# Seven-product groups of a squared-ReLU layer: another order of the sums of quarters and of the matmuls around each read of a partial sum

**Chip, cores, metric.** One core of one Trainium2 chip (trn2). The metric is the device time of one execution in microseconds (us), medians of several runs; lower is better.

## The reference

```python
def _attn_ref(x, filt_r, filt_i):                  # x: 8 x 3008 x 256
    X = np.fft.rfft(x, axis=1)
    Y = X * (filt_r + 1j * filt_i)[None]
    return np.fft.irfft(Y, n=x.shape[1], axis=1).astype(np.float32)

def _moe_ref(x, w_in, w_out):                      # x: 24064 x 256, d_ff 2048
    h = np.maximum(x @ w_in, 0.0)
    return (h * h @ w_out).astype(np.float32)
```

A filter in the frequency domain along the sequence, then a layer with squared ReLU. The output is float32.

## The kernel before

The layer runs over 47 groups (0 to 46) of 512 tokens. Each group has eight steps. A step makes two 128-row blocks of h by four matmuls of 512 columns (**first product**, L562), ScalarE takes the ReLU out of PSUM (L566) and VectorE squares it (L570). The **second product** of a group runs in the eight steps of the next group, behind each step's first product, and so do the parts of the Fourier transform of a later batch. For groups 40 to 45 the second product isn't made plainly (64 matmuls of 256 columns) but as a 2 x 2 product of quarters by seven products P1 to P7 (Strassen's scheme in Winograd's form), of 16 matmuls of 128 columns each: 7/8 of the work, for four sums of quarters of h on VectorE.

```python
    # p_x16 has 4 buffers, PSUM tag psO 2; a11..a22 are the quarters of h in SBUF (float16)
    def sums(g, k):                       # called in step k of the next group, on VectorE
        a11, a12, a21, a22 = quads(g)
        if k == 0:
            t = p_x16.tile([128, 8, D], F16, tag="x16", name=f"s3_{g}")
            nc.vector.tensor_sub(out=t, in0=a11, in1=a21)
            sg[g] = {1: a11, 2: a12, 4: a22, 5: a21, 7: t}
        elif k == 1:
            nc.vector.tensor_add(out=a21, in0=a21, in1=a22)
        elif k == 2:
            t = p_x16.tile([128, 8, D], F16, tag="x16", name=f"s2_{g}")
            nc.vector.tensor_sub(out=t, in0=a21, in1=a11)
            sg[g][6] = t
        elif k == 4:
            ...                           # t = a12 - sg[g][6], operand of P3

    # which matmuls of which product stand behind which step: (product, from, to)
    PARTS = (((1, 0, 16),), ((2, 0, 14),), ((2, 14, 16), (5, 0, 8), (6, 0, 4)),
             ((6, 4, 16), (5, 8, 10)), ((5, 10, 16), (7, 0, 8)), ((7, 8, 16),), ((4, 0, 16),),
             ((3, 0, 16),))

    def products(g, k):                   # part k, one step later than sums
        f = sg[g]
        for p, m0, m1 in PARTS[k]:
            ...                           # f["x"], f["y"]: two PSUM tiles of tag psO
            o = f["x"][:, 0] if p in (1, 6, 7, 4) else f["y"][:, 0 if p == 2 else 1]
            for m in range(m0, m1):
                q, t = divmod(m, 2)
                nc.tensor.matmul(o[:, t, :], f[p][:, q, 128*t:128*t+128], sg["w"][p][:, q, :],
                                 start=(m == 0 and p in (1, 2)), stop=(q == 7), ...)
            if m1 < 16:
                continue
            if p == 1:   nc.scalar.copy(out=f["pu"][:, 0], in_=o)      # partial sum read
            elif p == 6: nc.scalar.copy(out=f["u2"], in_=o)            # partial sum read
            elif p == 7:
                nc.scalar.copy(out=f["pu"][:, 1], in_=o)               # partial sum read
                ...                                                    # tiles top, bot
                nc.vector.tensor_add(out=f["top"][..., 0:128], in0=f["y"][:, 0], in1=f["pu"][:, 0])
                nc.vector.tensor_add(out=f["bot"][..., 128:256], in0=f["y"][:, 1], in1=f["pu"][:, 1])
            elif p == 4: ...              # ScalarE: bot[..., 0:128] = o; store
            elif p == 3: ...              # VectorE: top[..., 128:256] = o + u2; store

    for s in range((NG + 1) * SLOTS):     # NG = 47 groups, SLOTS = 8 steps
        g, k = divmod(s, SLOTS)
        if g < NG: ffn_g1(g, k)           # first product and ReLU
        ...
        if (s - 1) // SLOTS - 1 in SEVEN: products((s - 1) // SLOTS - 1, (s - 1) % SLOTS)
        ...                               # plain second product for the other groups
        if g - 1 in SEVEN: sums(g - 1, k)
        if g < NG: ffn_sq(g, k)           # square
```

P1, P6, P7 and P4 add one after the other into the same PSUM region and are read in between: the next may not add before ScalarE has copied what is there. P2 is alone in its region; P3 adds onto P5.

## Time and profile before

| | before |
|---|---|
| time, median (range, 4 runs) | 793.6 us (793.36 to 793.72) |
| TensorE busy, VectorE, ScalarE | 98%, 74%, 70% of the span |
| steady late group, P6 to the next group's P6 | 13.86 us |
| of that, TensorE's work by its issue rate | 13.17 us |

The third row is the distance between equal rows of TensorE's timeline; the fourth counts matmuls times their distance from start to start. The lines are in the prediction. In them L638, L641, L644 and L648 are the four sums in VectorE's queue; L666 is every matmul of the seven products; L676 and L678 are ScalarE's copies behind P6 and P7; L681, L682 and L687 are VectorE's adds (top, bot, top).

### The profile page before, as it was taken

How to read it: one execution, taken by the hardware profiler on the slowest of the kernel's cores; microseconds unless marked ns; L12 is line 12 of the kernel's file. 1: busy time of each engine (PE TensorE's matmuls, PEld its weight loads, DVE VectorE, ACT ScalarE, POOL GpSimd, SP SyncE). 2: the span in 40 equal slices, each digit the busy share in tenths (PEclk: the TensorE clock that was granted, in tenths of full speed). 3: DMA queues.
4: the chain of work that ended last, by engine and by line, in shares of the span. 5: the costliest groups of instructions: out<-in, count | busy, mean ns of one | idle time of the engine just before them, and what ended most of it. 6: DMA issues, size and time to landing. Idle time of an engine off the chain costs nothing.

```text
span 793.1 us, 15477 instructions
## 1 busy us (share of the span) xinstructions
PE 778.2 (98%) x6390; PEld 553.3 (70%) x6390; DVE 584.3 (74%) x943; ACT 558.6 (70%) x723; POOL 23.6 (3%) x36
## 2 busy tenths in 40 slices
PE   8989999999999999999999999999999999999998
PEld 5846667667676676867777677776767667676666
DVE  6856995579855897559965699556995579778773
ACT  3966777777777676767777677676777777776663
POOL 3800000000000000000000000000000000000000
PEclk9999999999999999999999999999999999999999
DMA  9994554345724467155472555524663332511011
GB/s 362 368 260 139 146 158 121 88 132 161 195 65 109 158 165 181 39 170 140 129 177 57 171 146 147 121 75 153 158 178 88 94 133 67 139 36 54 29 54 54
DMA packets 88574, 107.36 MB, mean 135 GB/s; under 512 B 6336, under 2 KB 79040, under 8 KB 84288
## 3 DMA queue, kind: packets, MB, share of 16 engines
q1 hardware_dynamic: 88296, 106.19, 46.8%
q8 instruction: 50, 0.82, 0.4%
q10 hardware_dynamic: 144, 0.18, 0.1%
q14 instruction: 20, 0.16, 0.1%
q0 software_dynamic: 64, 0.00, 0.0%
HBM read 58.12 MB, written 48.23 MB: 134 GB/s over the span
## 4 chain that ended last, share of the span: by engine, by line
PE 86%; DVE 10%; ACT 2%; DMA 1%; issue 0%; SPq 0%; ACTq 0%; DVEq 0%
PE psH L562 36%; PE psO L579 34%; PE psA L361 3%; DVE h L570 2%; PE psY L532 2%; PE psB L445 2%; PE psP L496 2%; PE psX L666 2%; DVE prod L453 2%; ACT h L566 1%; PE psY L666 1%; PE warm L268 1%; DVE s L644 1%; DVE h L641 1%; DVE s L638 1%; DMA zt<-dZ 1%
## 5 line engine op out<-in xcount | busy, mean ns | idle before, releaser
L566 ACT ACTIVATE h<-psH 128x1024 f16<-128x1024 f32 x376 | 384.9, 1025 | 186.6 <-PE psH L562 183.4
L562 PE MATMUL psH<-yt,sWin 128*128 128x512 f16 (+7 forms) x1728 | 387.4, 351 | 1.4 <-DVE yt L541 0.7
L579 PE MATMUL psO<-sWout,h 128*128 128x256 f16 x2624 | 339.2, 272 | 0.6 <-DVE h L570 0.6
L579 PEld LDWEIGHTS <-h 128*128 128x128 f16 x2624 | 253.2, 98 | 65.9 <-DVE h L570 0.9
L570 DVE TENSOR_TENSOR h<-h 128x1024 f16<-128x1024 f16 x376 | 251.8, 684 | 63.2 <-ACT h L566 62.5
L562 PEld LDWEIGHTS <-sWin 128*128 128x128 f16 x1728 | 157.8, 98 | 101.0 <-issue 3.8
L453 DVE TENSOR_TENSOR prod<-psB,sF 128x1024 f16<-128x1024 f32 x84 | 102.3, 1218 | 2.8 <-PE psB L445 2.8
L541 DVE CAST yt<-psY 128x376 f16<-128x376 f32 x62 | 34.0, 549 | 56.8 <-PE psY L532 56.6
L367 DVE CAST u<-psA 96x512 f16<-96x512 f32 x50 | 34.3, 687 | 47.3 <-PE psA L361 45.1
L498 ACT CAST ze<-psP 128x512 f16<-128x512 f32 x84 | 49.1, 585 | 17.2 <-PE psP L496 14.7
L590 ACT COPY ost<-psO 128x512 f32<-128x512 f32 (+1 forms) x84 | 48.8, 581 | 7.9 <-DMA out_dram<-bot 4.3
L532 PE MATMUL psY<-sC,zt 112*128 112x94 f16 x512 | 43.1, 207 | 1.6 <-DMA zt<-dZ 1.6
L532 PEld LDWEIGHTS <-zt 112*128 112x128 f16 x512 | 35.5, 99 | 11.7 <-issue 1.8
L467 DVE TENSOR_TENSOR yf<-prod,yf 128x512 f16<-128x512 f16 x84 | 35.7, 425 | 2.9
L361 PE MATMUL psA<-x,sC 94*96 94x512 f16 x96 | 36.6, 382 | 0.0
L445 PE MATMUL psB<-ut,sSB 128*128 128x256 f16 x192 | 36.5, 273 | 0.0
L539 ACT CAST yt<-psY 128x376 f16<-128x376 f32 x66 | 30.9, 468 | 2.8 <-issue 2.0
L496 PE MATMUL psP<-yf,sSP 128*128 128x256 f16 x168 | 32.1, 272 | 0.5 <-DVE prod L453 0.3
L445 PEld LDWEIGHTS <-sSB 128*128 128x128 f16 x192 | 18.4, 98 | 19.5
L666 PEld LDWEIGHTS <-h 128*128 128x128 f16 x384 | 24.0, 98 | 7.6 <-issue 2.0
L340 DVE CAST x<-x 94x2048 f16<-94x2048 f32 x24 | 29.2, 1216 | 0.0
L365 ACT CAST u<-psA 96x512 f16<-96x512 f32 x50 | 28.6, 572 | 0.0
(88 smaller groups left out, 394.0 us busy)
## 6 DMA issues: line engine op xcount, KB each, us to landing
x<-in_x_dram SPq DMA_DIRECT2D x20, 768.0 KB
zt<-dZ SPq DMA_DIRECT2D x64, 192.0 KB
dU<-u SPq DMA_DIRECT2D x28, 384.0 KB
dZ<-ze SPq DMA_DIRECT2D x28, 384.0 KB
out_dram<-ost SPq DMA_DIRECT2D x58, 128.0 KB
ut<-dU SPq DMA_DIRECT2D x7, 1024.0 KB
out_dram<-ost SPq DMA_DIRECT2D x27, 256.0 KB
xw<-in_x_dram SPq DMA_DIRECT2D x6, 1024.0 KB
```

What stands on the lines that cost most here:

```text
L361: nc.tensor.matmul(ps[0:96, :], sSA, x16s[(b, c)][:, m, :], start=True, stop=True)
L445: nc.tensor.matmul(ps[:, i * D:(i + 1) * D], sSB[:, 2 * p + i, :], uts[b][:, 2 * p + i, :], start=True, stop=True)
L453: nc.vector.tensor_mul(out=prod, in0=ps.rearrange("p (a d) -> p a d", d=D).unsqueeze(1).to_broadcast([128, 2, 2, D]), in1=sF[:, :, 2 * p:2 ...
L496: nc.tensor.matmul(ps[:, i * D:(i + 1) * D], sSP[:, 2 * p + i, :], yf[:, i, :], start=True, stop=True)
L498: nc.scalar.copy(out=zes[(b, c)][:, 2 * i6:2 * i6 + 2, :], in_=ps.rearrange("p (a d) -> p a d", d=D))
L532: nc.tensor.matmul(ps[:, 94 * jj:94 * jj + 94], zt[:, 4 * (g % 2) + jj, dt * 128:(dt + 1) * 128], sSY, start=True, stop=True)
L562: nc.tensor.matmul(ps[:, i, o:o + n], sWin[:, dt, jt * 128:(jt + 1) * 128], yts[b][:, dt, r:r + n], start=(dt == 0), stop=(dt == 1))
L566: nc.scalar.activation(out=h2[:, 2 * s:2 * s + 2, :], in_=ps, func=AF.Relu)
L570: nc.vector.tensor_mul(out=v, in0=v, in1=v)
L579: nc.tensor.matmul(pso[g][:, t % 2, :], h2s[g][:, jt, t * 128:(t + 1) * 128], sWout[:, jt, :], start=(jt == 0), stop=(jt == NJT - 1))
L590: nc.scalar.copy(out=ost[:, h0:h0 + step, :], in_=pso[g][:, h0:h0 + step, :])
L666: nc.tensor.matmul(o[:, t, :], f[p][:, q, 128 * t:128 * t + 128], sg["w"][p][:, q, :], start=(m == 0 and p in (1, 2)), stop=(q == 7), skip ...
```

## The change

Its intent: P5's and P6's sums are to be ready earlier, by making a21+a22 first (in a buffer of its own, since a21 is still needed), and behind each read of a partial sum other matmuls are to stand in TensorE's program ("fillers"), so that ScalarE's copy is over when the region is needed again. The VectorE adds move from P7 to P2, which now ends last of the two.

```diff
         if k == 0:
-            t = ...; nc.vector.tensor_sub(out=t, in0=a11, in1=a21)      # operand of P7
+            nc.vector.tensor_add(out=t, in0=a21, in1=a22); f[5] = t     # t: a new tile each time
         elif k == 1:
-            nc.vector.tensor_add(out=a21, in0=a21, in1=a22)             # operand of P5, in place
+            nc.vector.tensor_sub(out=t, in0=f[5], in1=a11); f[6] = t
         elif k == 2:
-            t = ...; nc.vector.tensor_sub(out=t, in0=a21, in1=a11)      # operand of P6
+            nc.vector.tensor_sub(out=t, in0=a11, in1=a21); f[7] = t
 ...
-    PARTS = (((1, 0, 16),), ((2, 0, 14),), ((2, 14, 16), (5, 0, 8), (6, 0, 4)),
-             ((6, 4, 16), (5, 8, 10)), ((5, 10, 16), (7, 0, 8)), ((7, 8, 16),), ((4, 0, 16),),
-             ((3, 0, 16),))
+    PARTS = (((1, 0, 16),), ((2, 0, 12), (5, 0, 2)), ((5, 2, 8), (6, 0, 8)),
+             ((6, 8, 16), (5, 8, 14)), ((5, 14, 16), (7, 0, 16)), ((2, 12, 16), (4, 0, 8)),
+             ((4, 8, 16), (3, 0, 4)), ((3, 4, 16),))
 ...
             elif p == 7:
                 nc.scalar.copy(out=f["pu"][:, 1], in_=o)
+            elif p == 2:
                 f["top"] = ...; f["bot"] = ...; (the two tensor_add)
```

More of the change, by code (lines that the diff above doesn't have):

```diff
@@ L633, in sums @@
     def sums(g, k):
+        if k not in (0, 1, 2, 4):
+            return
         a11, a12, a21, a22 = quads(g)
         if k == 0:
-            t = p_x16.tile([128, 8, D], F16, tag="x16", name=f"s3_{g}")
-            nc.vector.tensor_sub(out=t, in0=a11, in1=a21)
-            sg[g] = {1: a11, 2: a12, 4: a22, 5: a21, 7: t}
-        elif k == 1:
-            nc.vector.tensor_add(out=a21, in0=a21, in1=a22)
-        elif k == 2:
-            t = p_x16.tile([128, 8, D], F16, tag="x16", name=f"s2_{g}")
-            nc.vector.tensor_sub(out=t, in0=a21, in1=a11)
-            sg[g][6] = t
-        elif k == 4:
-            t = p_x16.tile([128, 8, D], F16, tag="x16", name=f"s4_{g}")
-            nc.vector.tensor_sub(out=t, in0=a12, in1=sg[g][6])
-            sg[g][3] = t
-    PARTS = (((1, 0, 16),), ((2, 0, 14),), ((2, 14, 16), (5, 0, 8), (6, 0, 4)),
-             ((6, 4, 16), (5, 8, 10)), ((5, 10, 16), (7, 0, 8)), ((7, 8, 16),), ((4, 0, 16),),
-             ((3, 0, 16),))
+            sg[g] = {1: a11, 2: a12, 4: a22}
+        f = sg[g]
+        t = p_x16.tile([128, 8, D], F16, tag="x16", name=f"sum_{g}_{k}")
+        if k == 0:
+            nc.vector.tensor_add(out=t, in0=a21, in1=a22)
+            f[5] = t
+        elif k == 1:
+            nc.vector.tensor_sub(out=t, in0=f[5], in1=a11)
+            f[6] = t
+        elif k == 2:
+            nc.vector.tensor_sub(out=t, in0=a11, in1=a21)
+            f[7] = t
+        else:
+            nc.vector.tensor_sub(out=t, in0=a12, in1=f[6])
+            f[3] = t
+    PARTS = (((1, 0, 16),), ((2, 0, 12), (5, 0, 2)), ((5, 2, 8), (6, 0, 8)),
+             ((6, 8, 16), (5, 8, 14)), ((5, 14, 16), (7, 0, 16)), ((2, 12, 16), (4, 0, 8)),
+             ((4, 8, 16), (3, 0, 4)), ((3, 4, 16),))
     def products(g, k):
```

## The prediction

> **What bounds the kernel now.** I read the page first, then the chain of work that ended last, then each engine's timeline of one late group.
>
> The page, part 1 and part 4:
>
> ```profile
> PE 778.2 (98%) x6390; PEld 553.3 (70%) x6390; DVE 584.3 (74%) x943; ACT 558.6 (70%) x723; POOL 23.6 (3%) x36
> ...
> PE 86%; DVE 10%; ACT 2%; DMA 1%; issue 0%; SPq 0%; ACTq 0%; DVEq 0%
> ```
>
> TensorE is 98% busy and 86% of the chain, so most of the time nothing but fewer matmuls can help. But 10% of the chain is on VectorE. In the chain by order of time, nearly all of that lies after 698 us, in the six late groups (40 to 45) whose second product is made of seven products of quarters, the only part that the change touches. Call them P1 to P7; each has 16 matmuls of 128 columns, in eight parts, one behind each of the eight first-product steps of the next group.
>
> TensorE's timeline of one such group in its steady state (start, length, engine, line, op, operands, count, idle):
>
> ```profile
> 733.15 0.40 PE L666 MATMUL psX<-sT,s 128*128 128x128 f16 x4 [0.30 <-DVE s L644]
> 733.39 1.03 PE L562 MATMUL psH<-yt,sWin 128*128 128x512 f16 x4
> ...
> 737.54 0.61 PE L666 MATMUL psX<-sT,s 128*128 128x128 f16 x8
> 737.99 1.03 PE L562 MATMUL psH<-yt,sWin 128*128 128x512 f16 x4
> 739.08 1.05 PE L666 MATMUL psX<-sT,h 128*128 128x128 f16 x16
> ...
> 745.99 0.28 PE L666 MATMUL psY<-sWout,h 128*128 128x128 f16 x2
> 746.10 0.61 PE L666 MATMUL psY<-sT,h 128*128 128x128 f16 x8
> 747.01 0.40 PE L666 MATMUL psX<-sT,s 128*128 128x128 f16 x4 [0.30 <-DVE s L644]
> ```
>
> Here starts are to be read, not lengths, since ends are modelled and overlap. From 733.15 to 747.01 one group takes 13.86 us. The work: four 512-column matmuls take 0.865 us from start to next start, so 32 take 6.92; 12 of 128 columns take 0.67, so 112 take 6.25. Sum 13.17. The other 0.69 us is two holes. The first: the eight of P5 start at 746.10 and would be issued by 746.55 (8 x 0.0557), but P6 starts at 747.01: 0.46 us. The second: the first-product step of 737.99 is issued by 738.85, but P4 starts at 739.08: 0.23 us. The profile doesn't mark this second hole as idle at all, because the modelled end (739.02) covers it.
>
> What ends the first hole, VectorE's timeline:
>
> ```profile
> 741.93 0.42 DVE L687 TENSOR_TENSOR top<-psY,u 128x256 f32<-128x256 f32 x1 [1.13 <-PE psY L666]
> 742.27 1.21 DVE L638 TENSOR_TENSOR s<-h 128x2048 f16<-128x2048 f16 x1
> 743.40 0.68 DVE L570 TENSOR_TENSOR h<-h 128x1024 f16<-128x1024 f16 x1
> 744.00 1.22 DVE L641 TENSOR_TENSOR h<-h 128x2048 f16<-128x2048 f16 x1
> 745.14 0.68 DVE L570 TENSOR_TENSOR h<-h 128x1024 f16<-128x1024 f16 x1
> 745.74 1.22 DVE L644 TENSOR_TENSOR s<-h 128x2048 f16<-128x2048 f16 x1
> ```
>
> The first line is the add that ends the previous group; it had to wait for P3. Behind it stand three sums with two squares between, 1.74 us from sum to sum (1.13 + 0.60), and P6 needs the third. It ends at 746.96, and P6 starts 0.05 us later.
>
> What ends the second hole, ScalarE's timeline:
>
> ```profile
> 737.74 1.02 ACT L566 ACTIVATE h<-psH 128x1024 f16<-128x1024 f32 x1 [0.62 <-PE psH L562]
> 738.66 0.37 ACT L678 COPY pu<-psX 128x256 f32<-128x256 f32 x1
> ```
>
> The copy of the partial sum behind P7 stands behind a 0.92 us activation and ends at 739.03; P4 adds into the same PSUM and starts at 739.08. Only one step of 0.86 us lies between P7 and P4 as cover.
>
> **What the Trainium skill says.** "TensorE: Matmul & The Clock Gate", section "Wait — 56ns, not 53.3ns?", gives 55.6 and 215.7 ns from start to start at 128 and 512 columns; the trace agrees (0.67/12 = 55.8, 0.865/4 = 216). "PSUM — Partial Sum Buffer", section "Engine vs sequencer instructions", says that matmuls start and complete in program order: a matmul that waits holds up all behind it, so useful work must be put ahead of it in the program. The trace agrees: nothing fills the two holes. "VectorE: DVE Perf Modes", section "Side-by-side: where the cycles go for N=2048 bf16", gives about 1224 ns at two elements a cycle; these sums take 1212 to 1219 ns, in place (1217) or to another buffer (1215), so a buffer of its own costs nothing. "Perfetto Trace Analysis", section "Tensor Engine Instruction (MATMUL, LD_WEIGHTS)", says that a matmul's end is estimated; the unmarked second hole agrees.
>
> **The change part by part.** The order of instructions built from the changed kernel has the same counts as before on every engine, 12782 rows on TensorE and 817 on VectorE, so no work is added or removed. I place events from T, the start of the first-product step behind P3 (741.73 above).
>
> *Sums.* a21+a22 is made first, minus a11 second, a11-a21 third. VectorE starts sums at T+0.54, T+2.27, T+4.01, as now, so they are ready at T+1.80, T+3.53, T+5.27. TensorE reaches P5 at 0.86 + 0.89 + 0.87 + 0.67 = T+3.29 (step, P1, step, 12 of P2): 1.5 us to spare. It reaches P6 after two of P5, a step and six of P5, 0.11 + 0.86 + 0.33 more: T+4.59 against T+3.53, so 1.06 us to spare. The 0.46 us hole closes. The chain to P6 gets one sum and one square shorter (1.74 us) while P6 comes 0.22 us earlier by program order.
>
> *Fillers.* P7 now ends in the sixth part, and a step (0.86) and four of P2 (0.22) stand before P4. The copy ends 0.61 us behind the end of P7 (its start is held up by the activation and by the latency of about 0.2 us), and TensorE needs 1.08: 0.47 us to spare. The 0.23 us hole closes. P7 itself waits for the copy behind P6: from the end of the fourth step, the activation starts 0.20 later, the copy 0.92 after that, 0.37 long, 0.04 to the wait: 1.53. TensorE comes at 0.45 + 0.33 + 0.865 + 0.11 = 1.755, so 0.22 us to spare, the least of all. P3 waits for VectorE's add on P5, which now follows P2: done 0.20 + 0.34 + 0.42 + 0.05 = 1.01 us behind P2's end (latency, the add before it, its own length, the wait), wanted 0.45 + 0.86 + 0.45 = 1.76 behind it (half of P4, a step, the other half).
>
> *First late group* (40) has the inverse transform's last matmuls between. Its holes, computed alike: 704.89 - (703.83 + 0.45) = 0.61 and 711.36 - (710.27 + 0.875) = 0.22, together 0.83. There too the second sum (702.64) precedes P6 (704.04 by program order), and P7 has about 0.2 us to spare.
>
> *The last group* pays something back. Behind P3 of group 45 comes the ordinary second product of group 46, whose first PSUM buffer is freed by ScalarE's copy of P4. Now P4 is issued late enough to hide that. Afterwards TensorE arrives 0.45 + 0.22 + 0.67 = 1.34 us behind the last step; the copy ends 0.20 + 0.92 + 0.37 + 0.04 = 1.53. A new wait of 0.19 us.
>
> Sum: 5 x 0.69 + 0.83 - 0.19 = **4.1 us**, and TensorE is the end of the chain until the last copy and store, which don't change. 793.5 - 4.1 = **789.4 us**, 0.5% faster.
>
> **Rivals.** First, *another wait takes the place*: the 0.22 us before P7. If ScalarE were 0.3 us later than I place it, six times 0.1 us would come back, at most about 1 us if both copies slip; for it speaks the thin margin, against it that no record of these copies is over 0.03 us longer than its median in the steady groups. This would give 790 to 790.5. Second, *VectorE becomes the bound*: per group it has 8 squares at 0.60, four sums at 1.13 and three adds at about 0.36, 10.4 us of the new 13.17, and its idle of 1.13 us before the add for P3 stays, so I think not; if the chain from P3 through the sums still set the period, the gain would be only that of the second hole, 6 x 0.23 = 1.4 us, and the time 792.1. Third, *the clock*: a TensorE without holes could be throttled. The table by stretches of time shows TensorE 14.00 of 14.00 us busy at clock 1.00 before the late groups, so it isn't likely. Fourth, *the end hides it*: the stores of the last tiles could set the end. The chain shows TensorE up to 789.61, then 0.37 us of ScalarE and some 3 us for the last store, so whatever TensorE saves is saved. A bigger gain is not there to be had: all the holes together are 4.3 us.
>
> **Range and chances.** The holes are measured and the margins mostly over 0.4 us, so the range is narrow: 788.9 (all holes closed, no new wait, and a run 0.2 us under the median, as the spread of before is 793.36 to 793.7) to 790.4 (a thin margin lost). Over 2% needs 15.9 us, nearly four times all the holes. Faster 0.005, within 2% 0.99, slower 0.005.
>
> **What would show it.** Right: a steady period of 13.15 to 13.25 us from P6 to P6; no wait of TensorE on a sum; P4 starting one step and four matmuls behind P7 without a hole; span about 789.0. The new wait of about 0.2 us before the first second-product matmul of group 46. Wrong: a period above 13.4, with a hole before P7 (ScalarE's copy behind P6) or before P5 or P6 (VectorE's sums), or a lower granted clock after 698 us.

## The result, and the profile after

789.31 us (789.29 to 789.56, 4 runs) against 793.6: 4.3 us less. The ratio is 0.9947 (95% interval 0.993 to 0.9964). A ratio here is the mean time of one kernel's fast runs over that of the other's of the same rounds, so not quite the ratio of the medians. By the threshold of 2% this is "the same", and it lies inside the predicted range.

From the page of the changed kernel, its busy times and its chain by engine:

```profile
PE 774.9 (98%) x6390; PEld 552.6 (70%) x6390; DVE 584.4 (74%) x943; ACT 558.5 (71%) x723; POOL 23.6 (3%) x36
...
PE 91%; DVE 6%; ACT 1%; DMA 1%; issue 0%; ACTq 0%; SPq 0%; DVEq 0%
```

The work is the same, but VectorE's share of the chain is 6% where it was 10%. After 698 us the chain before has 31 us on VectorE and 8 on ScalarE; the chain after has nothing of VectorE there, and ScalarE only at the very end. TensorE's timeline of one steady group (lines have moved: L670 is now the seven products; same columns as in the prediction):

```profile
729.19 0.61 PE L670 MATMUL psX<-sT,sum 128*128 128x128 f16 x8
729.63 1.03 PE L562 MATMUL psH<-yt,sWin 128*128 128x512 f16 x4
...
732.14 0.28 PE L670 MATMUL psY<-sT,sum 128*128 128x128 f16 x2
732.25 1.06 PE L670 MATMUL psX<-sT,sum 128*128 128x128 f16 x16
733.15 1.03 PE L562 MATMUL psH<-yt,sWin 128*128 128x512 f16 x4
734.01 0.39 PE L670 MATMUL psY<-sWout,h 128*128 128x128 f16 x4
734.23 0.61 PE L670 MATMUL psX<-sT,h 128*128 128x128 f16 x8
...
742.35 0.61 PE L670 MATMUL psX<-sT,sum 128*128 128x128 f16 x8
```

From P6 (729.19) to the next P6 (742.35) are 13.16 us: the work alone. P7 at 732.25 follows the step and the last two of P5 without a gap, P4 at 734.23 the four of P2. VectorE and ScalarE in the same group:

```profile
737.95 0.42 DVE L692 TENSOR_TENSOR top<-psY,u 128x256 f32<-128x256 f32 x1 [0.46 <-PE psY L670]
738.29 1.22 DVE L643 TENSOR_TENSOR sum<-h 128x2048 f16<-128x2048 f16 x1
739.42 0.68 DVE L570 TENSOR_TENSOR h<-h 128x1024 f16<-128x1024 f16 x1
740.02 1.22 DVE L646 TENSOR_TENSOR sum<-sum,h 128x2048 f16<-128x2048 f16 x1
```

```profile
731.62 0.37 ACT L680 COPY u<-psX 128x256 f32<-128x256 f32 x1
732.34 1.02 ACT L566 ACTIVATE h<-psH 128x1024 f16<-128x1024 f32 x1 [0.36 <-PE psH L562]
733.35 0.37 ACT L682 COPY pu<-psX 128x256 f32<-128x256 f32 x1
```

The second sum ends at 741.24, and P6 starts at 742.35: the sum isn't waited for any more. The copy behind P6 ends at 731.99, P7 starts at 732.25; the copy behind P7 ends at 733.72, P4 starts at 734.23.

Where the time came from, by equal rows of the two timelines:

| stretch of TensorE | before | after | less |
|---|---|---|---|
| P1 of group 40 to P1 of group 41 | 699.61 to 714.87 = 15.26 | 697.87 to 712.29 = 14.42 | 0.84 |
| each of the next four groups | 13.86 | 13.16 | 0.70 |
| P1 of group 45 to the last group's second product | 770.31 to 782.45 = 12.14 | 764.93 to 776.56 = 11.63 | 0.51 |
| all of it | 82.84 | 78.69 | 4.15 |

The two profiles' spans differ by more, 793.1 - 787.2 = 5.9 us. The other 1.7 us stand ahead of the late groups: P1 of group 40 starts 1.74 us earlier after. This isn't the change. In the profiled run of before (795.18 us, 1.6 over the median) two things came together near 48 us. The transfer that the inverse transform's first matmul waits for came 0.59 us later (that matmul starts at 48.34, after the change at 47.75), and the granted clock fell to one half for a while, as the table of engines by stretches of time shows. Its columns are the stretch, its length, the busy time (and instructions) of PE, PEld, DVE, ACT and POOL, the granted clock, the share of DMA and GB/s. Before, then after:

```profile
48.00:50.00 2.00, 1.67 (x20) 1.70 (x21) 0.55 (x1) 0.57 (x2) 0.00 (x0) 0.56 1.09 358
50.00:52.00 2.00, 1.94 (x10) 0.74 (x9) 0.55 (x1) 0.37 (x1) 0.00 (x0) 0.59 1.06 228
```

```profile
48.00:50.00 2.00, 1.72 (x24) 1.11 (x21) 1.10 (x2) 0.94 (x2) 0.00 (x0) 1.00 1.05 337
```

Half clock for (0.44 + 0.41) x 2 / 0.5 = 3.4 us. The traces separate the two: from that first matmul to P1 of group 40 it is 650.10 to 650.12 us in the six profiled runs at full clock with the same six groups (after, e1, e3, e5, e12, e13), and 651.27 to 651.52 in the four with a spell (before, e2, e4, e6). So of the 1.74 us here 1.15 are the half clock and 0.59 the later transfer. Such a spell comes in some runs of nearly every kernel here, makes them 1.2 to 1.8 us longer than the kernel's other runs (medians) and shows as a mean clock of 0.998 or 0.997 for the run. So below I give, beside the median, the runs without it ("full clock": 1.0), and read differences of a few tenths from rows of the traces.

### The profile page after: what moved, and what is told of

Same layout as the page of the kernel before. It is cut to its first block, busy times and chain, and to the rows that moved or that the text cites. A ratio compares the mean times of both kernels' runs of the same rounds, so it can differ in the third digit from the quotient of the medians.

```text
span 787.2 us, 15477 instructions
## 1 busy us (share of the span) xinstructions
PE 774.9 (98%) x6390; PEld 552.6 (70%) x6390; DVE 584.4 (74%) x943; ACT 558.5 (71%) x723; POOL 23.6 (3%) x36
## 4 chain that ended last, share of the span: by engine, by line
PE 91%; DVE 6%; ACT 1%; DMA 1%; issue 0%; ACTq 0%; SPq 0%; DVEq 0%
PE psH L562 39%; PE psO L579 34%; PE psX L670 3%; PE psA L361 3%; PE psY L532 2%; PE psB L445 2%; PE psP L496 2%; PE psY L670 2%; DVE prod L453 2%; DVE h L570 2%; PE warm L268 1%; DMA wout<-in_moe_w_out_dram 1%; PE psf L287 1%; PE psf L290 1%; DVE yf L467 0%; ACT sF L298 0%
## 5 line engine op out<-in xcount | busy, mean ns | idle before, releaser
L579 PEld LDWEIGHTS <-h 128*128 128x128 f16 x2624 | 253.3, 98 | 66.0 <-DVE h L570 0.9
L670 PEld LDWEIGHTS <-sum 128*128 128x128 f16 x384 | 23.8, 98 | 4.9
```

What stands on the lines that cost most here:

```text
L579: nc.tensor.matmul(pso[g][:, t % 2, :], h2s[g][:, jt, t * 128:(t + 1) * 128], sWout[:, jt, :], start=(jt == 0), stop=(jt == NJT - 1))
L670: nc.tensor.matmul(o[:, t, :], f[p][:, q, 128 * t:128 * t + 128], sg["w"][p][:, q, :], start=(m == 0 and p in (1, 2)), stop=(q == 7), skip ...
```

## The experiments

Each had five rounds (e7 six runs). The kernel before, run on the same chips, had full-clock runs of 793.35 to 794.3 us and runs with a spell of 795.06 to 795.42. All results were correct.

**e1: the sums alone.** The new `sums`, the old `PARTS`, the adds at P7 again.

```diff
 (changed kernel)
-    PARTS = (((1, 0, 16),), ((2, 0, 12), (5, 0, 2)), ...
+    PARTS = (((1, 0, 16),), ((2, 0, 14),), ((2, 14, 16), (5, 0, 8), (6, 0, 4)), ...   # as before
```

> The new sums (a21+a22 first, in its own buffer) with the old order of parts. My theory (two separate holes, one owed to the third sum in VectorE's queue, one to ScalarE's copy behind P7): the hole before P6 closes (0.46 x 5 + 0.61 = 2.9 us), the 0.23 us hole before P4 stays. Expected 793.6 - 2.9 = 790.7 us, steady period 13.4. Rival (the order of parts does the work, the sums have slack enough): 793 or more. Rival (the sums do all of it): 789.3.

Measured: median 790.68 us (full clock 790.35, 790.6, 790.68), ratio 0.9964. TensorE's timeline:

```profile
730.01 0.39 PE L670 MATMUL psX<-sT,sum 128*128 128x128 f16 x4
...
734.84 1.03 PE L562 MATMUL psH<-yt,sWin 128*128 128x512 f16 x4
735.93 1.05 PE L670 MATMUL psX<-sT,h 128*128 128x128 f16 x16
...
743.40 0.39 PE L670 MATMUL psX<-sT,sum 128*128 128x128 f16 x4
```

The period is 13.39 us, and the hole before P4 (735.93 - 734.84 - 0.865 = 0.23) is the same as before. The order of the sums is worth 2.9 of the 4.3 us.

**e2: the parts alone.** The new `PARTS`, with the adds behind P2, which ends last in it, and the old `sums` (first a11-a21, then a21+a22 in place, then P6's).

> The new order of parts with the old sums (a11-a21 first, a21+a22 second in place, the operand of P6 third). My theory: the hole before P4 closes (0.23), but P5 is now reached at T+3.29 and its sum is ready at T+3.53 (hole 0.24), and P6 then at T+4.83 against T+5.27 (hole 0.44): steady period 13.17 + 0.68 = 13.85, as before, and with the 0.2 us wait at the last group 793.6 to 793.9 us. Rival (the fillers are what helps): about 792.2 (six times 0.23 less) or lower.

Measured: full-clock runs 793.78 and 793.88 us, three runs with a spell at 795.25 to 795.37 (median 795.25); ratio 1.0009 (0.9997 to 1.0022). TensorE's timeline:

```profile
730.47 0.83 PE L666 MATMUL psY<-sWout,h 128*128 128x128 f16 x12
731.40 0.29 PE L666 MATMUL psY<-sT,h 128*128 128x128 f16 x2
731.52 1.03 PE L562 MATMUL psH<-yt,sWin 128*128 128x512 f16 x4
732.39 0.50 PE L666 MATMUL psY<-sT,h 128*128 128x128 f16 x6
733.14 0.62 PE L666 MATMUL psX<-sT,s 128*128 128x128 f16 x8 [0.25 <-DVE s L644]
```

P5 starts 0.93 us behind P2's twelve, whose issue takes 0.67: a hole of 0.26 for its sum. P6 starts 0.75 behind six of P5, which take 0.33: a hole of 0.42. The hole before P4 is gone, but the period is 13.86 again (719.28 to 733.14). The new order of parts alone gains nothing, since it asks for the sums sooner; with the new sums in place it gains about 1.3 us more (e1's full-clock runs against 789.3). The single parts (2.9 and 0) don't add up to the whole: the second works only with the first.

**e3: first, but in place.** a21+a22 is made first but written over a21, and P7's operand, a11-a21, is got as a22 - (a21+a22-a11).

```diff
-        t = p_x16.tile([128, 8, D], F16, tag="x16", name=f"sum_{g}_{k}")
+        t = a21 if k == 0 else p_x16.tile([128, 8, D], F16, tag="x16", name=f"sum_{g}_{k}")
...
-            nc.vector.tensor_sub(out=t, in0=a11, in1=a21)
+            nc.vector.tensor_sub(out=t, in0=a22, in1=f[6])
```

> The changed kernel, but the first sum is written in place over a21, and a11-a21 is computed as a22 minus the second sum, which is equal but for rounding. Tells apart 'made first' from 'in its own buffer'. My theory: only the order counts, so 789.3 us within 0.2 and the same period 13.16. Rival (the buffer of its own counts: an in-place write is slower or makes someone wait): over 790.

Measured: full-clock runs 789.35 and 789.54 us (median of all 789.88), ratio 0.9954, period 13.16 (716.00 to 729.16). So it is "first" that counts; the buffer of its own is only what makes "first" possible with the old formula, and this formula does without it.

**e4: no filler between P6 and P7.** The second half of P5 moves behind P7.

```diff
-             ((6, 8, 16), (5, 8, 14)), ((5, 14, 16), (7, 0, 16)), ((2, 12, 16), (4, 0, 8)),
+             ((6, 8, 16),), ((7, 0, 16),), ((5, 8, 16), (2, 12, 16), (4, 0, 8)),
```

> The changed kernel with the second half of P5 moved from between P6 and P7 to behind P7, so only one first-product step lies between the end of P6 and P7. Same work. My theory: the copy behind P6 is done 0.20+0.92+0.37+0.04 = 1.53 us behind the step before it, TensorE arrives at 0.45+0.865 = 1.32: a hole of 0.21 before P7, six times 1.3 us, so 790.6 us and a period of 13.37. Rival (the fillers don't matter, the step alone covers the copy): 789.3.

Measured: 790.72 and 790.96 us (mean clock 0.999, without the cost of a spell) and three runs with a spell at 792.43 to 792.84; ratio 0.9974. Between the step and P7:

```profile
733.18 1.03 PE L562 MATMUL psH<-yt,sWin 128*128 128x512 f16 x4
734.27 1.05 PE L670 MATMUL psX<-sT,sum 128*128 128x128 f16 x16
```

1.09 us for a step of 0.865: a hole of 0.225, 0.21 expected; period 13.39 (718.03 to 731.42). The profile marks no idle here either. The fillers between P6 and P7 are worth their 1.3 us.

**e5: no filler between P7 and P4.**

```diff
-             ... ((2, 12, 16), (4, 0, 8)),
+             ... ((4, 0, 8), (2, 12, 16)),
```

> The changed kernel with the four matmuls of P2 moved from ahead of the first half of P4 to behind it: no filler but the step between P7 and P4. My theory: not these four fillers but the place of P7's end closes the hole. P7 now ends 1.00 us behind its step, so TensorE reaches P4 at 1.00+0.865 = 1.87 against 1.53 for the copy: 0.3 us to spare, no hole, 789.3 us. Rival (the fillers are needed, as the change's words suggest): up to six times 0.22 back, 790.6.

Measured: full-clock runs 789.67, 789.67 and 789.96 us, ratio 0.9952, period 13.16 (716.42 to 729.58), P4 0.86 behind the step (720.38 to 721.24): no hole, and the copy behind P7 ends 0.28 ahead of it (720.96). Here the filler isn't needed. What closed the hole of before is that P7 ends a whole product (16 matmuls) behind its step, when the activation of that step is nearly over, where before it was half a product (eight).

**e6: the last group's tiles swapped.** In the last group the first tile of the second product takes the free PSUM tag.

```diff
-        if s % 4 == 0:                        pso[g] = psO(...)
-        elif g == NG - 1 and half == 0:       pso[g] = psF(...)
+        if g == NG - 1 and s % 4 == 0:        pso[g] = psF(...)
+        elif s % 4 == 0 or (g == NG - 1 and half == 0):  pso[g] = psO(...)
```

> The changed kernel, in which the last group's second product takes the free PSUM tag for its first tile and the one that the seven products leave for its second. My theory: the 0.2 us wait at 776.36 to 776.56 goes, 789.1 us. Rival (the end is set by the last stores or by ScalarE): 789.3, no change.

Measured: 789.25 us (mean clock 0.999) and four runs with a spell, 790.74 to 790.98; median 790.84, ratio 0.9955. The times don't decide; TensorE's timeline does. Changed kernel, then e6:

```profile
775.47 1.06 PE L670 MATMUL psY<-sWout,sum 128*128 128x128 f16 x16
776.56 7.15 PE L579 MATMUL psO<-sWout,h 128*128 128x256 f16 x64
```

```profile
777.22 1.06 PE L670 MATMUL psY<-sWout,sum 128*128 128x128 f16 x16
778.11 7.15 PE L579 MATMUL psO<-sWout,h 128*128 128x256 f16 x64
```

16 matmuls are issued in 0.89 us. The changed kernel needs 1.09, e6 0.89: the predicted wait of 0.2 us existed and is gone. From P1 of group 40 to this row e6 takes 78.49 us, the changed kernel 78.69.

**e7: group 39 by seven products too.** e6 with the range begun one group earlier; the sums of weights are made two steps before group 40.

```diff
-    SEVEN = range(40, NG - 1)
+    SEVEN = range(39, NG - 1)
...
-        if s == SEVEN[0] * SLOTS:
+        if s == 40 * SLOTS - 2:
```

> As the last one, and group 39 is made by seven products too (its weights' sums made two steps before group 40). A plain late group is 32 x 0.2163 + 64 x 0.1095 = 13.93 us of TensorE, one of seven products without holes 13.17. Expected 789.1 - 0.75 = 788.4 us. Rival (VectorE, with more to do for group 39 beside the inverse transform's casts, opens new holes): 789 or more.

Measured: 788.74 to 791.5 us, median 790.47; full-clock runs 789.13 and 790.14, and the fastest, 788.74, at a mean clock of 0.999 without the cost of a spell; ratio 0.9949. No clear gain over e6. TensorE's timeline has one new wait, and none on the sums:

```profile
691.72 0.33 PE L532 MATMUL psY<-sC,zt 112*128 112x94 f16 x4 [0.78 <-DMA zt<-dZ]
```

The last batch's inverse transform waits for its operand's transfer, which does not come sooner because group 39 is shorter. My theory for e7 was wrong, and so was its rival: neither the full gain nor holes on VectorE's account.

**e10: the last batch's inverse transform one step later** (on top of e7).

```diff
-            put((38 if b == 1 else 45) + n // 2, n % 2, unit_y, b, n)
+            put((38 if b == 1 else 46 if b == B - 1 else 45) + n // 2, n % 2, unit_y, b, n)
```

> As e7, with the last batch's inverse transform put one step later, because e7's trace showed TensorE waiting 0.78 us (0.93 from start to start) for its operand's transfer when group 39 became shorter. My theory (e7's gain was eaten by this wait alone): the wait goes or shrinks, and group 39 gives its 0.75 us: runs at full clock 788.4 us, runs with a half-clock spell near 48 us some 1.5 more, about 790.0. Rival (VectorE can't carry group 39's sums): holes before P5 or P6 of group 39 in the trace, full-clock runs at 789.1 or more.

Measured: full-clock runs 789.38 and 789.41 us, three with a spell at 790.46 to 790.6; ratio 0.9951. The wait for the transfer is gone, but one step on, the first product waits for the result of the transform just made later (it had started at 694.55 with two matmuls of 64 columns, about 0.1 us, so the hole is some 0.5 us):

```profile
695.18 0.97 PE L562 MATMUL psH<-yt,sWin 128*128 128x448 f16 x6 [0.40 <-ACT yt L539]
```

From the forward transform's last pair of matmuls (psB, 676.38) to the last group's second product (776.88) are 100.50 us, against 677.45 to 778.11 = 100.66 in e6. So group 39 gives 0.16 of the 0.75 us that were expected of it (0.73 by the rows of e9 below): most of the rest is this new hole. Whether another place for the transform would free it stays open.

**e9: no seven-product groups at all,** in the kernel before.

> The kernel before without any seven-product group (all groups by the plain second product). Asks what the seven products were worth before the change. A plain group is 13.93 us against 13.86 of the kernel before with its holes: five times 0.07, less 0.08 in group 40. Expected 793.6 + 0.2 = 793.8 us, so the saved matmuls had been given back in the two holes. Rival (the seven products were worth their full 0.75 us each before): 798.

Measured: 793.38 to 793.88 us, median 793.51, all at full clock, beside 793.53 to 794.3 of the kernel before at full clock in the same rounds; ratio 0.9993 (0.9981 to 1.0005). The same row of two plain groups, one after the other:

```profile
711.99 1.03 PE L562 MATMUL psH<-yt,sWin 128*128 128x512 f16 x4
725.89 1.03 PE L562 MATMUL psH<-yt,sWin 128*128 128x512 f16 x4
```

A plain group takes 13.90 us (13.93 expected), one of seven products 13.17 without its holes. So before the change the six groups by seven products were worth nothing that these runs can show: of the 0.73 us of TensorE's work saved in each, 0.69 was given back in the two holes. The change didn't save work; it made the earlier saving count.

**e11 and e12: TensorE kept busy in a wait near 47 us.** Twenty more matmuls of zeros where TensorE waits 1.0 to 1.6 us for the first transfer of the inverse transform, on top of e10 and of e6.

```diff
-            for k in range(2):
+            for k in range(22 if n == 0 else 2):      # 128-column matmuls of zeros
```

> As e10, and twenty matmuls of zeros more (20 x 0.056 = 1.1 us) where TensorE waits 1.0 to 1.6 us for the first transfer of the inverse transform, at 46.5 to 48.2 us. Asks where the 1.5 us come from by which runs of one kernel differ: in those runs the granted clock is one half for 3.41 us right behind this wait. If the wait brings the spell on, no run has it, and all five lie within 0.4 us of 788.4. Rival (the spell comes by chance or from elsewhere): it stays in two or more of the five runs, 790.0.

> The changed kernel with the last group's tiles swapped (as e6) and the twenty matmuls of zeros in the wait at 46.5 us (as e11), without group 39. If both readings hold: no run has a half-clock spell near 48 us, and all five lie within 0.4 us of 789.1. Rival (no spell in e11's five runs was luck): spells in two or more of the five, at about 790.6.

**e13: the changed kernel again,** on the same chip as e12.

> The changed kernel itself, on the same chip as e12, for a direct comparison. Full-clock runs at 789.3 us, 0.2 over e12's; runs with the half-clock spell, if it has some as the kernel before does (in 3 of 9), at about 790.9. Rival (the changed kernel is free of the spell, as its first four runs were): all five at 789.3.

Measured: e11 788.69 to 789.52 us, median 789.16, ratio 0.9938; e12 789.11 to 789.74, median 789.27, ratio 0.9942; no run of either shows the cost of a spell (one of e11 has a mean clock of 0.999, and is its fastest). e13: full-clock runs 789.2, 790.03 and 790.12, two with a spell at 791.06 and 791.46, median 790.12, ratio 0.9958. So the changed kernel isn't free of the spell, as its first four runs had been. None in ten runs with the zeros, against three in five of e10 (e11's chip) and two in five of e13 (e12's chip) without, fits the wait as the cause; but the kernel before had none in its nine runs on e12's chip, and e9 none in five on another, so it is likely, not shown. The length of the wait alone doesn't decide it: the profiles with a spell show marked waits of 1.53 to 1.62 us and one of 1.07 (e2), those with neither a spell nor the zeros 1.00 to 1.24 and one of 1.53 (e10). Nor does the spell always stand right behind the wait: it begins about when the wait ends (before) or up to 2 us later (e6). Only one run of e11 lies within 0.4 us of the 788.4 expected, since group 39 gave little, as in e10; four of e12's five lie within 0.4 of 789.1. e12 beats the changed kernel by 0.85 us in the medians here, and by 0.76 in the medians of the full-clock runs. The traces account for 0.2 of it (from P1 of group 40 to the last group's second product, 698.22 to 776.72 = 78.50 in e12 and 697.77 to 776.47 = 78.70 in e13); the rest I can't place, and in the two profiled runs it isn't there (e13's span is 0.3 us the shorter). In those two, e12's transfer near 48 us came 0.46 us later (48.12 against 47.66), which hides the 0.2; whether it also made the 0.9 us between e13's full-clock runs isn't known, since only one was profiled.

## Why the prediction was right

*Two holes and their sizes.* Right: 13.86 to 13.16 a group where 13.17 was worked out. e1 and e4 each leave or reopen one such hole and get 13.39; e2 puts the same 0.69 back in other places.

*The first hole is owed to the third sum in VectorE's queue.* Right, by e1 (closes with the order of sums alone), e2 (stays with it) and e3 (the buffer plays no part). The second sum was predicted ready 1.06 us ahead of P6; its end stands 1.11 ahead, less 0.05 for the wait.

*The second hole is owed to ScalarE's copy behind an activation.* Right, with one correction from e5. The prediction gave the step and the four of P2 as the cover; the four could be left out. The arithmetic of the prediction had it (0.47 to spare, of which the four are 0.22), but its words did not.

*The thin margin before P7.* Predicted 0.22 us to spare; the copy ends 0.26 before P7, less 0.04 for the wait. It held in each group, and e4 shows what it guards: 0.225 us a group once the fillers are gone.

*Group 40 and the end.* 0.83 predicted, 0.84 measured; a new wait of 0.19 predicted, 0.20 measured and taken away by e6. The sum was 4.1 us; the late groups show 4.15, the run times 4.3.

*The rivals.* No wait of TensorE on sums or copies is left in the late groups. VectorE didn't become the bound. The clock stayed at 1.00 there. The end hid nothing. One side remark was wrong: that VectorE's wait of 1.13 us before the add for P3 stays. It is 0.46 now, as the squares fall differently; nothing hung on it.

*Two readings that don't stand,* though nothing hung on them. The prediction puts nearly all of VectorE's 10% of the chain (10% of the span, some 79 us) after 698 us; only 31 us lie there, and the chain after still has 6% on VectorE, all ahead of the late groups. And its 12782 and 817 rows are counts of the built program, which the record doesn't hold; the pages have 6390 matmuls, as many weight loads and 943 VectorE instructions on both sides.

*What the prediction didn't see* is the spell of half clock, which falls on some runs of either kernel. Its one failed sign comes from there: the "span about 789.0" is 4.1 off the 793.1 of a run with a spell, and the span came out at 787.2. The spell is ahead of the late groups and no part of the change, but it is bigger than several of the effects studied here, and the two profiles alone would have given 5.9 us for the change.

## What to carry to other kernels

On an engine that is 98% busy, look for holes by start-to-start times against the issue rate, not by marked idle time: one of the two here wasn't marked at all. A saving of work on the bounding engine can be worth nothing until its new operands come early enough, so order the side engine's queue by when each result is first needed, and place a partial sum's end late behind the step whose activation delays the copy. When parts of a change are tried one at a time, one that gains nothing alone (e2) can still carry a third of the whole.

## What the Trainium skill lacked or had wrong

- "TensorE: Matmul & The Clock Gate", section "HAM oscillation — how this bites in real kernels", gives the rule as no idle gaps over about 3.4 us (the section after it adds frequent short idles, without a length). Here the clock was halved for 3.4 us in five profiled runs with a marked wait of only 1.07 to 1.62 us, ended by a transfer, shortly before; none of ten runs had it with 1.1 us of matmuls of zeros in that wait. That this shorter wait brings it on is likely, not proved: e10's profile has a wait of 1.53 us and no halving.
- "PSUM — Partial Sum Buffer", section "The four PSUM rules", says that a synchronised read of a partial sum in the middle of an accumulation group is allowed, but not what it costs TensorE. Here: 0.20 us from the last matmul's issue, 0.37 for ScalarE's copy of 128x256, 0.04 to the next matmul, 0.61 in all, and up to 0.92 more if an activation stands before it in ScalarE's queue.
- No page says by how much marked idle time understates a hole in TensorE's row: 0.46 us was marked as 0.30, and 0.23 and 0.225 weren't marked.
